# Scores of two blocks by row halves in turn, packed loads for short chunks, and two held conversions

## The chip, the cores and the metric

One core of one Trainium2 chip runs the whole program. The metric is the device time of one execution in microseconds (us); the median of several runs counts.

## The reference

Three steps, in this order, on a batch of 4 sequences of 576 tokens with 8 heads of 64:

```python
# 1. retention: attention with a decay in place of the softmax
scores = scale * (q @ k.T)
gamma = 1.0 - 2.0 ** (-5.0 - head)
ret = scores * where(i >= j, gamma ** (i - j), 0)
x = (ret @ v).reshape(2304, 512)
# 2. first feed-forward block, w_in 512x2048, w_out 2048x512
h = x @ w_in
y = (h * cos(h)) @ w_out
# 3. second feed-forward block, the same sizes
h = y @ w_in2
g = where(h >= 1, h, where(h <= -1, 0, (h + 1) ** 2 / 4))
out = g @ w_out2
```

The four weight matrices arrive with 64-bit elements; q, k and v are fp32.

## The kernel before, in words

**Precision.** The products of the feed-forward blocks are made of three matmuls each: every operand is split into a high and a low part (tiles with a leading index of 2, types fp32r), and high x high, high x low and low x high are added up. The weights are converted on the chip from the two 32-bit halves of each element. `begin` (L127) makes a scaled copy X of the upper half on ScalarE (L134); `convert` (L145) makes C from both halves on VectorE (L150 to L156), has `signed` (L139 to L143) work on X and W, copies the high part out on ScalarE (L158) and makes the low part on VectorE (L159). Raw weights come in by `load_raw` (L112) on the queue of SyncE (SP), into rotating buffers `raw` and `rsh` of two each; a later raw load waits until the conversion that reads the buffer is through.

**Chunks and blocks.** The 2304 tokens are cut into 5 blocks of 256, 512, 512, 512 and 512 tokens (L25) and, within sequences and blocks, into 20 chunks of 128 or 64 tokens (L49). Chunks 4, 6, 14 and 15 have 64 tokens: two in block 1, two in block 3. Blocks 0 and 1 together hold chunks 0 to 6, block 2 holds 7 to 10, block 3 holds 11 to 15 and block 4 holds 16 to 19.

**One chunk** (class `Chunk`, L251). `load` (L261) fetches q and k, transposed so that pairs of heads lie on 128 rows, then k and v by tokens, then a table of decays `pt`; for chunk 0 the last two go out on ScalarE's queue, otherwise all three on SP's. `prep` (L276) scales v by a table, on ScalarE in eight small copies for block 1 (L281), on VectorE for the others (L283). `scores` (L285) makes for each of four pairs of heads two matmuls over 64 rows each: the upper row half (j = 0) into PSUM bank S, the lower (j = 1) into bank O (in the start also y0 to y3; the profile names them bkS, bkO, bky). A fp32 matmul is two passes in the profile, so 16 per chunk. `masked` (L293) multiplies both banks with the mask on VectorE (R, L300). `full` (L305) then uses the two banks again for the carried state and for the state update, `inner` (L318) multiplies with v, `state` (L327) updates the state T, and `post` (L339) scales the result by `pt` into xs and splits it into the high and low part of x. So bank S comes free when the state is updated and bank O when xs is made.

**Order of the work.** The start (L640 to L680) loads chunks 0 to 6 and the first raw weights, then goes through the chunks; matmuls on zeros (`warm`, L633) fill TensorE early on. The conversion of the first W_in tile is called for after chunk 2 (L676), of the first W_out tile after chunk 4 (L678). From L740 on a loop over slots, each one column block of the hidden layer of one token block, runs the first product (`mm1`, L367), the activation, and two slots later the second product (`mm2`, L379). The chunks of blocks 2 to 4 are laid into the slots of the block before them by a plan (L586 to L621). The second feed-forward block follows at L774. The program's order sets priorities only: a scheduler of the framework walks each engine's instructions with its own estimate of their times and may put a ready one ahead of an earlier one that isn't. An order is forced with `behind(later, earlier)` (L94), which adds a dependency without a wait on the chip where both are on the same engine.

```python
for p in range(NP):
    for j in range(2):
        js = slice(j * D, (j + 1) * D)
        self.lastpe = PE.matmul(self.Z[j][:n, p * P:p * P + n], self.qk[js, 1, p, :n], self.qk[js, 0, p, :n], start=True, stop=True)
```

Of the kernel before, what the change touches and what calls it, by code (L numbers as in the profile page):

```python
# [13 lines left out]
AF = mybir.ActivationFunctionType  # L14
ALU = mybir.AluOpType
# [3 lines left out]
B, H, S, D = 4, 8, 576, 64  # L19
NT, DM, DFF = B * S, H * D, 2048  # L20
P = 128
KB = DM // P
NP = H // 2
# [25 lines left out]
def _chunks():  # L49
    out = []  # L50
    for b in range(B):
        t = 0
        while t < S:
            o, w = BLOCKS[_block_of(b * S + t)]
            n = min(P, S - t, o + w - (b * S + t))
            out.append((b, t, n))
            t += n
    return out


CHUNKS = _chunks()
NCH = len(CHUNKS)
# [3 lines left out]
def retention_moe_kernel(ctx: ExitStack, tc: tile.TileContext, qk, kv, win1, wout1, win2, wout2, mask, vtab, ptab, out):  # L66
    nc = tc.nc
    V, A, G, SY, PE = nc.vector, nc.scalar, nc.gpsimd, nc.sync, nc.tensor
# [14 lines left out]
    vtb = const.tile([P, NCH, H], F32, tag="vtb", name="vtb")  # L83
# [7 lines left out]
    def f(t):  # L91
        return t.bitcast(F32)

    def behind(later, earlier):  # L94
        tc.add_manual_dep(later.ins, earlier.ins.name, mybir.DependencyInfo(mybir.DependencyClass.NoSync, mybir.DependencyReason.SCHED_ONLY), reason="pace")

    def bank(tag):
        return psy.tile([P, 512], F32, tag=tag, name="bk" + tag)
# [28 lines left out]
    def begin(L, i, c, after=None, late=False):  # L127
        raw, raw2 = raws.pop((L, i, c))
        hi = raw[:, :, 1].bitcast(F32)
        if late:  # L130
            X, W = [wp.tile([P, DM], F32, tag=f"wo{k}", name="XW"[k - 1]) for k in (1, 2)]
        else:
            X, W = [cv.tile([P, DM], F32, tag=k, name=k) for k in "XW"]
        i0 = A.activation(X, hi, AF.Copy, scale=2.0 ** -112)  # L134
        if after is not None:
            behind(i0, after)
        return raw, raw2, X, W, late
# [7 lines left out]
    def convert(begun, o, after=None):  # L145
        raw, raw2, X, W, late = begun
        lo, hi = raw[:, :, 0], raw[:, :, 1]
        C = wp.tile([P, DM], I32, tag="wo3", name="C") if late else cv.tile([P, DM], I32, tag="C", name="C")
        if raw2 is not None:
            i0 = V.tensor_scalar(out=C, in0=raw2.bitcast(I32)[:, 1:1 + 2 * DM:2], scalar1=7, scalar2=None, op0=ALU.logical_shift_left)  # L150
        else:
            i0 = V.tensor_scalar(out=C, in0=hi, scalar1=23, scalar2=None, op0=ALU.logical_shift_left)
        if after is not None:
            behind(i0, after)
        if raw2 is None:
            V.scalar_tensor_tensor(out=C, in0=lo, scalar=9, in1=C, op0=ALU.logical_shift_right, op1=ALU.bitwise_or)  # L156
        signed(hi, X, W, 1)
        A.activation(o[:, 0, :], W, AF.Copy)  # L158
        return V.scalar_tensor_tensor(out=o[:, 1, :], in0=C, scalar=2.0 ** -43, in1=X, op0=ALU.mult, op1=ALU.mult)  # L159
# [3 lines left out]
    def make_wi1(c, begun, after=None):  # L163
        t = wr.tile([P, 2, DM], F32R, tag="wi", name="wi")
        convert(begun, t, after)
        SY.dma_start(out=wd[0, 0, c], in_=f(t))
        wi[0, c] = t

    def make_wo1(c, begun, after=None):
        t = wp.tile([P, 2, DM], F32R, tag=f"wo{c}", name=f"wo{c}")  # L170
        convert(begun, t, after)
        wo[0, c] = t
# [69 lines left out]
    CH = {}  # L242
# [8 lines left out]
    class Chunk:  # L251
# [9 lines left out]
        def load(self, other=None, homes=None):  # L261

            n = self.n
            if homes is None:
                both = ap.tile([P, 4, DM], F32, tag="qkv", name="qkv")
                self.qk, self.kv = both[:, 0:2], both[:, 2:4]
                self.pt = ap.tile([P, NP, P], F32, tag="pt", name="pt")
            else:
                self.qk, self.kv = [p_.tile([P, 2, DM], F32, tag=g_, name="qkv") for p_, g_ in homes[:2]]
                self.pt = homes[2][0].tile([P, NP, P], F32, tag=homes[2][1], name="pt")  # L270
            self.qk = self.qk.rearrange("p a (i m) -> p a i m", i=NP)
            SY.dma_start(out=self.qk, in_=qk[self.i])
            (other or SY).dma_start(out=self.kv[:n], in_=kv[self.i][:n])
            (other or SY).dma_start(out=self.pt[:, :, :n], in_=ptab[:, :, self.t:self.t + n])

        def prep(self):  # L276
            n = self.n
            v = self.kv[:n, 1, :].rearrange("p (h d) -> p h d", h=H)
            if self.blk == 1:
                for h in range(H):  # L280
                    A.activation(v[:, h, :], v[:, h, :], AF.Copy, scale=vtb[:n, self.i, h:h + 1])  # L281
                return
            V.tensor_tensor(out=v, in0=v, in1=vtb[:n, self.i, :].unsqueeze(2).to_broadcast([n, H, D]), op=ALU.mult)  # L283

        def scores(self):  # L285
            n = self.n
            self.Z = [bank(t) for t in self.banks]
            for p in range(NP):
                for j in range(2):
                    js = slice(j * D, (j + 1) * D)  # L290
                    self.lastpe = PE.matmul(self.Z[j][:n, p * P:p * P + n], self.qk[js, 1, p, :n], self.qk[js, 0, p, :n], start=True, stop=True)

        def masked(self, home=None):  # L293
            n = self.n
# [44 lines left out]
        def post(self):  # L339
            n = self.n  # L340
            xs = ap.tile([P, NP, P], F32, tag="xs", name="xs", bufs=1)
            V.tensor_tensor(
                out=xs[:, :, :n], in0=self.Z[1].rearrange("p (i m) -> p i m", i=NP)[:, :, :n],
                in1=self.pt[:, :, :n], op=ALU.mult)
            if self.off == 0:
                new_x(self.blk, BLOCKS[self.blk][1])
            xx = xhl[self.blk]
            os_ = slice(self.off, self.off + n)
            A.activation(xx[0][:, :, os_], xs[:, :, :n], AF.Copy)
            return V.tensor_tensor(out=xx[1][:, :, os_], in0=xs[:, :, :n], in1=f(xx[0][:, :, os_]), op=ALU.subtract)  # L350
# [272 lines left out]
    first = members[0] + members[1]  # L623
# [37 lines left out]
    for k, i in enumerate(first):  # L661
        c = CH[i]
        c.scores()
        c.masked((None, "wo2")[k % 2])
        if k < 2:
            warm(10, c.lastpe)
        if k + 1 < len(first):
            CH[first[k + 1]].prep()
        c.full()
        c.inner()  # L670
        c.state()
        if k < 2:
            warm(10, c.lastpe)
        lastpost = c.post()
        if k == 2:
            make_wi1(0, begin(0, 0, 0))  # L676
        if k == 4:
            make_wo1(0, begin(0, 1, 0))  # L678
            load_raw(0, 1, 1)
    make_wi1(1, begin(0, 0, 1))  # L680
    for p in range(-9, 0):
# [58 lines left out]
    for s in range(N1):  # L740
# [7 lines left out]
        after = lastpost if s <= pos_of[1, 0] else None  # L748
# [19 lines left out]
        q = 2 * (s - N1)  # L768
# [5 lines left out]
    for t, (sb, q, k) in enumerate(steps):  # L774
# [6 lines left out]
        n = 0  # L781
# [10 lines left out]
def _layout(q, k, v, moe_w_in, moe_w_out, moe2_w_in, moe2_w_out):  # L792
    import numpy as np

    qk = np.zeros((NCH, P, 2, NP, P), q.dtype)
    kv = np.zeros((NCH, P, 2, DM), q.dtype)
    for i, (b, t, n) in enumerate(CHUNKS):
        for j, a in enumerate((q, k)):
            qk[i, :, j, :, :n] = a[b, :, t:t + n, :].reshape(NP, 2, n, D).transpose(1, 3, 0, 2).reshape(P, NP, n)
        for j, a in enumerate((k, v)):  # L800
            kv[i, :n, j, :] = a[b, :, t:t + n, :].transpose(1, 0, 2).reshape(n, DM)

    def bits(w):
        w = np.ascontiguousarray(w)
        return w.view(np.int64)

    def wi(w):
        return bits(w.reshape(KB, P, NC, P).transpose(2, 1, 0, 3).reshape(NC, P, DM))

    def wo(w):  # L810
        return bits(w.reshape(NC, P, DM))

    g = np.array(GAMMA, np.float64)
    i = np.arange(S)
    start = np.array([t for b, t, n in CHUNKS])
    mask = np.triu(np.ones((P, P), np.float32))
    j = np.arange(P)[:, None, None] + start[None, :, None]
    vtab = (g[None, None, :] ** (-j)).astype(np.float32)
    pw = (g[:, None] ** i[None, :] / 8.0).astype(np.float32)
    ptab = np.repeat(pw.reshape(NP, 2, 1, S), D, axis=2).reshape(NP, P, S).transpose(1, 0, 2)  # L820
    return dict(qk=qk, kv=kv, win1=wi(moe_w_in), wout1=wo(moe_w_out), win2=wi(moe2_w_in), wout2=wo(moe2_w_out),
                mask=mask, vtab=vtab, ptab=ptab)

# [26 lines left out]
```

## Time and profile before

| | |
|---|---|
| median of 3 runs | 898.96 us (896.07 to 900.01) |
| the profiled execution | 897.41 us |
| its span, first to last instruction | 895.6 us |
| TensorE matmul busy (PE) | 869.6 us, 97% |
| TensorE weight load busy (PEld, beside PE) | 746.9 us, 83% |
| VectorE busy (DVE) | 632.2 us, 71% |
| ScalarE busy (ACT) | 481.8 us, 54% |
| mean granted TensorE clock | 0.991 of full |

The profile names an instruction by engine, line (L291 is line 291 of the kernel), operation and tiles, as out<-in. PE is TensorE's matmul, PEld its weight load, DVE VectorE, ACT ScalarE, POOL GpSimd; SPq and ACTq are the queues on which SyncE and ScalarE issue transfers. "idle before <-releaser" is how long an engine stood before an instruction and what released it. Matmuls are pipelined, so their durations overlap; the distance of their starts is what one costs.

### The profile page before, as it was taken

How to read it: one execution, taken by the hardware profiler on the slowest of the kernel's cores; microseconds unless marked ns; L12 is line 12 of the kernel's file. 1: busy time of each engine (PE TensorE's matmuls, PEld its weight loads, DVE VectorE, ACT ScalarE, POOL GpSimd, SP SyncE). 2: the span in 40 equal slices, each digit the busy share in tenths (PEclk: the TensorE clock that was granted, in tenths of full speed). 3: DMA queues.
4: the chain of work that ended last, by engine and by line, in shares of the span. 5: the costliest groups of instructions: out<-in, count | busy, mean ns of one | idle time of the engine just before them, and what ended most of it. 6: DMA issues, size and time to landing. Idle time of an engine off the chain costs nothing.

```text
span 895.6 us, 13569 instructions
## 1 busy us (share of the span) xinstructions
PE 869.6 (97%) x4876; PEld 746.9 (83%) x4876; DVE 632.2 (71%) x1152; ACT 481.8 (54%) x925; POOL 105.6 (12%) x82
## 2 busy tenths in 40 slices
PE   7888999999999999999999999999999999999997
PEld 6776888788888778788888899888888989898896
DVE  4797999765877785968889477685745667555554
ACT  3577988653566664666776644343433435423333
POOL 0022322200212221222232200000000000000000
PEclk9899999999999999999999999999999999999999
DMA  9968898855595968575986787676766765766431
GB/s 316 348 209 290 302 315 313 289 188 157 186 305 206 344 235 318 186 262 180 356 294 229 257 270 244 239 257 190 232 189 197 237 189 192 242 193 185 153 94 71
DMA packets 78114, 211.80 MB, mean 236 GB/s; under 512 B 9696, under 2 KB 21728, under 8 KB 78048
## 3 DMA queue, kind: packets, MB, share of 16 engines
q1 hardware_dynamic: 77088, 210.01, 69.8%
q10 hardware_dynamic: 960, 0.93, 0.3%
q8 instruction: 39, 0.64, 0.3%
q14 instruction: 27, 0.22, 0.1%
HBM read 170.02 MB, written 40.89 MB: 235 GB/s over the span
## 4 chain that ended last, share of the span: by engine, by line
PE 80%; DVE 7%; DMA 3%; ACT 3%; issue 2%; SPq 0%; DVEq 0%; ACTq 0%
PE hq L512 19%; PE h L376 14%; PE bky L391 6%; PE bky L392 6%; PE bky L393 6%; PE bky L565 5%; PE bky L564 5%; PE bky L566 5%; DVE W L142 1%; PE bkO L311 1%; PE bkO L376 1%; PE bkS L376 1%; PE bkS L565 1%; PE bkO L564 1%; PE bkO L324 1%
## 5 line engine op out<-in xcount | busy, mean ns | idle before, releaser
L512 PE MATMUL hq<-xc,wq 128*128 128x384 f32 x1008 | 198.4, 337 | 0.7 <-DVE sC L520 0.3
L376 PE MATMUL h<-xhl,wi 128*128 128x512 f32 (+1 forms) x864 | 194.2, 371 | 3.6 <-ACT wi L158 2.4
L512 PEld LDWEIGHTS hq<-xc,wq 128*128 128x128 f32 x1008 | 179.8, 188 | 12.8 <-DVE sC L520 0.6
L376 PEld LDWEIGHTS h<-xhl,wi 128*128 128x128 f32 x864 | 149.1, 189 | 33.2 <-ACT wi L158 3.5
L439 POOL TENSOR_TENSOR gl<-t,gh 128x512 fp32r<-128x512 f32 (+1 forms) x78 | 105.4, 1352 | 405.1 <-ACT gh L438 378.5
L438 ACT ACTIVATE gh<-t 128x384 fp32r<-128x384 f32 (+2 forms) x176 | 96.5, 549 | 56.0 <-DVE t L547 33.9
L546 ACT ACTIVATE t<-t,half 128x384 f32<-128x384 f32 x96 | 58.9, 615 | 107.2 <-DVE t L545 107.1
L391 PE MATMUL bky<-gh,wo 128*128 128x512 f32 x256 | 101.2, 395 | 2.4 <-ACT gh L438 2.4
L392 PE MATMUL bky<-gh,wo 128*128 128x512 f32 x256 | 100.1, 391 | 0.0
L393 PE MATMUL bky<-gl,wo 128*128 128x512 f32 x256 | 87.9, 390 | 0.0
L547 DVE TENSOR_TENSOR t<-t,sC 128x384 f32<-128x384 f32 x96 | 53.3, 556 | 33.3 <-ACT t L546 32.9
L564 PE MATMUL bky<-wo,gh 128*128 128x512 f32 x192 | 75.6, 394 | 0.2 <-ACT gh L438 0.2
L565 PE MATMUL bky<-wo,gh 128*128 128x512 f32 x192 | 75.6, 394 | 0.0
L431 ACT ACTIVATE t<-t 128x512 f32<-128x512 f32 (+1 forms) x80 | 46.9, 587 | 52.1 <-DVE t L426 51.9
L439 DVE TENSOR_TENSOR gl<-t,gh 128x384 fp32r<-128x384 f32 (+1 forms) x98 | 54.2, 556 | 18.0 <-ACT gh L438 17.8
L566 PE MATMUL bky<-wo,gl 128*128 128x512 f32 x192 | 61.0, 394 | 0.0
L545 DVE TENSOR_SCALAR t<-sC 128x384 f32<-128x384 f32 x96 | 34.4, 358 | 36.0 <-ACT sC L532 34.4
L391 PEld LDWEIGHTS bky<-gh,wo 128*128 128x128 f32 x256 | 48.0, 188 | 13.4 <-ACT gh L438 3.2
L392 PEld LDWEIGHTS bky<-gh,wo 128*128 128x128 f32 x256 | 48.1, 188 | 9.8 <-issue 0.3
L393 PEld LDWEIGHTS bky<-gl,wo 128*128 128x128 f32 x256 | 47.7, 188 | 9.7
L141 DVE TENSOR_SCALAR X<-X 128x512 int32<-128x512 int32 x64 | 30.7, 479 | 27.3 <-ACT X L134 27.1
L142 DVE SCALAR_TENSOR_TENSOR W<-raw,X 128x512 int32<-128x512 int32 x64 | 48.8, 762 | 1.1
(127 smaller groups left out, 1384.6 us busy)
## 6 DMA issues: line engine op xcount, KB each, us to landing
wq<-wq SPq DMA_DIRECT2D x72, 512.0 KB, 4.1
wi<-wd SPq DMA_DIRECT2D x48, 512.0 KB, 4.8
wo<-wd SPq DMA_DIRECT2D x48, 512.0 KB, 4.2
raw<-in_win_dram SPq DMA_DIRECT2D x32, 512.0 KB, 5.7
raw<-in_wout_dram SPq DMA_DIRECT2D x32, 512.0 KB, 5.6
qkv<-in_qk_dram SPq DMA_DIRECT2D x20, 512.0 KB, 6.3
wd<-wi SPq DMA_DIRECT2D x16, 512.0 KB, 4.4
wd<-cw SPq DMA_DIRECT2D x16, 512.0 KB, 5.5
```

Source lines behind the costliest of these rows:

```text
L142: V.scalar_tensor_tensor(out=Wi, in0=hi, scalar=-0x80000000, in1=Xi, op0=ALU.bitwise_and, op1=ALU.bitwise_or)
L376: PE.matmul(hp[s][:, :n], w[:, a, kb, :], x[b][:, kb, :], start=(i == 0), stop=(i == 3 * KB - 1))
L391: PE.matmul(o, w[:, 0, es], a, start=first and e % per == 0, stop=False, skip_group_check=True)
L392: PE.matmul(o, w[:, 1, es], a, start=False, stop=False, skip_group_check=True)
L393: PE.matmul(o, w[:, 0, es], b, start=False, stop=last, skip_group_check=True)
L438: A.activation(a, u, AF.Copy)
L439: eng.tensor_tensor(out=b, in0=u, in1=f(a), op=ALU.subtract)
L512: lastmm[0] = PE.matmul(o, w[:, a, kb, :], x[b][:, kb, :], start=first and i == 0, stop=i == 5, skip_group_check=True)
L546: A.activation(t, t, AF.Square, scale=0.5, bias=half)
L564: PE.matmul(y, a[:, js], w[:, 0, :], start=n == 0, stop=False)
L565: PE.matmul(y, a[:, js], w[:, 1, :], start=False, stop=False)
L566: PE.matmul(y, b[:, js], w[:, 0, :], start=False, stop=n == NC - 1)
```

## The change

- `load` takes q and k as one contiguous run of 2 x 4 x n elements per row, so a chunk of 64 tokens moves half of what it did; the decay table comes from an array with one packed copy per chunk, one run per row, where it was cut out of the whole table as four pieces of n elements.
- `prep` returns its last scaling for chunks of block 1.
- `scores` goes through the halves as (1, 0) instead of (0, 1), except in block 2, and puts each matmul behind the one before it, except in block 2.
- The first step (X) of the conversions called for after chunks 2 and 4 is put behind the last scaling of the next chunk, chunk 3 and chunk 5.
- The host's `_layout` lays out the arrays for it.

```diff
--- before.py
+++ after.py
@@ -268,27 +268,36 @@
             else:
                 self.qk, self.kv = [p_.tile([P, 2, DM], F32, tag=g_, name="qkv") for p_, g_ in homes[:2]]
                 self.pt = homes[2][0].tile([P, NP, P], F32, tag=homes[2][1], name="pt")
-            self.qk = self.qk.rearrange("p a (i m) -> p a i m", i=NP)
-            SY.dma_start(out=self.qk, in_=qk[self.i])
+
+            q = self.qk.rearrange("p a m -> p (a m)")[:, :2 * NP * n]
+            SY.dma_start(out=q, in_=qk[self.i][:, :2 * NP * n])
+            self.qk = q.rearrange("p (a i m) -> p a i m", a=2, i=NP)
             (other or SY).dma_start(out=self.kv[:n], in_=kv[self.i][:n])
-            (other or SY).dma_start(out=self.pt[:, :, :n], in_=ptab[:, :, self.t:self.t + n])
+            t = self.pt.rearrange("p i m -> p (i m)")[:, :NP * n]
+            (other or SY).dma_start(out=t, in_=ptab[self.i][:, :NP * n])
+            self.pt = t.rearrange("p (i m) -> p i m", i=NP)
 
         def prep(self):
             n = self.n
             v = self.kv[:n, 1, :].rearrange("p (h d) -> p h d", h=H)
             if self.blk == 1:
                 for h in range(H):
-                    A.activation(v[:, h, :], v[:, h, :], AF.Copy, scale=vtb[:n, self.i, h:h + 1])
-                return
+                    i0 = A.activation(v[:, h, :], v[:, h, :], AF.Copy, scale=vtb[:n, self.i, h:h + 1])
+                return i0
             V.tensor_tensor(out=v, in0=v, in1=vtb[:n, self.i, :].unsqueeze(2).to_broadcast([n, H, D]), op=ALU.mult)
 
         def scores(self):
             n = self.n
             self.Z = [bank(t) for t in self.banks]
+
+            self.lastpe = None
             for p in range(NP):
-                for j in range(2):
+                for j in (0, 1) if self.blk == 2 else (1, 0):
                     js = slice(j * D, (j + 1) * D)
+                    prev = self.lastpe
                     self.lastpe = PE.matmul(self.Z[j][:n, p * P:p * P + n], self.qk[js, 1, p, :n], self.qk[js, 0, p, :n], start=True, stop=True)
+                    if prev is not None and self.blk != 2:
+                        behind(self.lastpe, prev)
 
         def masked(self, home=None):
             n = self.n
@@ -341,7 +350,7 @@
             xs = ap.tile([P, NP, P], F32, tag="xs", name="xs", bufs=1)
             V.tensor_tensor(
                 out=xs[:, :, :n], in0=self.Z[1].rearrange("p (i m) -> p i m", i=NP)[:, :, :n],
-                in1=self.pt[:, :, :n], op=ALU.mult)
+                in1=self.pt, op=ALU.mult)
             if self.off == 0:
                 new_x(self.blk, BLOCKS[self.blk][1])
             xx = xhl[self.blk]
@@ -665,7 +674,7 @@
         if k < 2:
             warm(10, c.lastpe)
         if k + 1 < len(first):
-            CH[first[k + 1]].prep()
+            prepped = CH[first[k + 1]].prep()
         c.full()
         c.inner()
         c.state()
@@ -673,9 +682,9 @@
             warm(10, c.lastpe)
         lastpost = c.post()
         if k == 2:
-            make_wi1(0, begin(0, 0, 0))
+            make_wi1(0, begin(0, 0, 0, after=prepped))
         if k == 4:
-            make_wo1(0, begin(0, 1, 0))
+            make_wo1(0, begin(0, 1, 0, after=prepped))
             load_raw(0, 1, 1)
     make_wi1(1, begin(0, 0, 1))
     for p in range(-9, 0):
@@ -792,11 +801,11 @@
 def _layout(q, k, v, moe_w_in, moe_w_out, moe2_w_in, moe2_w_out):
     import numpy as np
 
-    qk = np.zeros((NCH, P, 2, NP, P), q.dtype)
+    qk = np.zeros((NCH, P, 2 * NP * P), q.dtype)
     kv = np.zeros((NCH, P, 2, DM), q.dtype)
     for i, (b, t, n) in enumerate(CHUNKS):
         for j, a in enumerate((q, k)):
-            qk[i, :, j, :, :n] = a[b, :, t:t + n, :].reshape(NP, 2, n, D).transpose(1, 3, 0, 2).reshape(P, NP, n)
+            qk[i, :, j * NP * n:(j + 1) * NP * n] = a[b, :, t:t + n, :].reshape(NP, 2, n, D).transpose(1, 3, 0, 2).reshape(P, NP * n)
         for j, a in enumerate((k, v)):
             kv[i, :n, j, :] = a[b, :, t:t + n, :].transpose(1, 0, 2).reshape(n, DM)
 
@@ -817,7 +826,10 @@
     j = np.arange(P)[:, None, None] + start[None, :, None]
     vtab = (g[None, None, :] ** (-j)).astype(np.float32)
     pw = (g[:, None] ** i[None, :] / 8.0).astype(np.float32)
-    ptab = np.repeat(pw.reshape(NP, 2, 1, S), D, axis=2).reshape(NP, P, S).transpose(1, 0, 2)
+    whole = np.repeat(pw.reshape(NP, 2, 1, S), D, axis=2).reshape(NP, P, S).transpose(1, 0, 2)
+    ptab = np.zeros((NCH, P, NP * P), np.float32)
+    for i, (b, t, n) in enumerate(CHUNKS):
+        ptab[i, :, :NP * n] = whole[:, :, t:t + n].reshape(P, NP * n)
     return dict(qk=qk, kv=kv, win1=wi(moe_w_in), wout1=wo(moe_w_out), win2=wi(moe2_w_in), wout2=wo(moe2_w_out),
                 mask=mask, vtab=vtab, ptab=ptab)
 
```

## Rows read from the trace of the kernel before

**Rows 1.** The page: the chain by engine, and one group of part 5.

```profile
PE 80%; DVE 7%; DMA 3%; ACT 3%; issue 2%; SPq 0%; DVEq 0%; ACTq 0%
...
L142 DVE SCALAR_TENSOR_TENSOR W<-raw,X 128x512 int32<-128x512 int32 x64 | 48.8, 762 | 1.1
```

**Rows 2.** Stretches: us, busy us of each engine (instructions), clock, DMA share, GB/s.

```profile
0.00:45.00 45.00, 35.82 (x436) 31.78 (x438) 28.67 (x58) 21.44 (x63) 1.22 (x5) 0.89 0.97 331
45.00:100.00 55.00, 47.49 (x269) 40.78 (x265) 48.86 (x95) 42.39 (x90) 14.12 (x9) 0.97 0.76 260
100.00:180.00 80.00, 76.71 (x436) 66.14 (x435) 71.46 (x122) 64.80 (x140) 22.46 (x19) 1.00 0.87 302
180.00:390.00 210.00, 209.62 (x1323) 168.86 (x1322) 157.52 (x275) 122.16 (x215) 36.85 (x27) 1.00 0.70 237
```

**Rows 3.** The same for the scores line L291 alone; last row sums 15 stretches.

```profile
211.10:213.05 1.95, 1.95 (x16) 1.83 (x16) 1.00 0.98 353
221.55:223.91 2.36, 2.21 (x16) 1.89 (x16) 1.00 0.60 153
243.56:243.97 0.41, 0.41 (x2) 0.29 (x2) 1.00 1.15 400
249.64:250.72 1.08, 1.08 (x14) 0.96 (x14) 1.00 0.91 322
267.60:268.21 0.61, 0.61 (x16) 0.54 (x16) 1.00 0.31 121
...
361.99:362.86 0.87, 0.87 (x12) 0.74 (x12) 1.00 0.00 0
...
383.04:383.69 0.65, 0.65 (x8) 0.52 (x8) 1.00 0.63 252
...
sum 12.81, PE 12.64 PEld 10.73; mean PE 0.84 PEld 0.72
```

**Rows 4.** Timeline of TensorE in two chunks of block 3: start, duration, instruction.

```profile
211.10 1.04 PE L291 MATMUL bkS<-qkv 64*128 64x128 f32 x7
...
212.18 0.94 PE L291 MATMUL bkO<-qkv 64*128 64x128 f32 x7
...
249.64 0.37 PE L291 MATMUL bkO<-qkv 64*128 64x128 f32 x1
249.64 0.37 PE L291 MATMUL bkS<-qkv 64*128 64x128 f32 x1
```

**Rows 5.** DMA queues from 0 to 45 us: packets, MB, share of 16 engines.

```profile
q1 hardware_dynamic: 6634, 13.88, 90.1%
q10 hardware_dynamic: 960, 0.93, 6.2%
```

**Rows 6.** Timeline of ScalarE from 0 to 50 us.

```profile
12.11 0.71 ACT L134 ACTIVATE X<-raw 128x512 f32<-128x512 f32 x1 [9.43 <-DMA raw<-in_win_dram]
...
19.83 2.02 ACT L281 ACTIVATE qkv<-qkv,vtb 128x64 f32<-128x64 f32 x8 [1.68 <-DMA qkv<-in_kv_dram]
...
26.88 0.65 ACT L134 ACTIVATE X<-raw 128x512 f32<-128x512 f32 x1
29.70 2.02 ACT L281 ACTIVATE qkv<-qkv,vtb 128x64 f32<-128x64 f32 x8 [2.17 <-DMA qkv<-in_kv_dram]
```

**Rows 7.** Two stretches, then rows of VectorE's, SP's and TensorE's timelines.

```profile
20.00:26.00 6.00, 2.57 (x48) 2.20 (x46) 1.11 (x3) 3.41 (x15) 0.00 (x0) 1.00 1.06 319
26.00:33.00 7.00, 5.97 (x52) 5.21 (x52) 6.89 (x15) 4.51 (x15) 0.00 (x0) 0.54 1.03 322
...
25.94 0.43 DVE L152 TENSOR_SCALAR C<-raw 128x512 int32<-128x512 int32 x1 [4.57 <-DMA raw<-in_wout_dram]
...
24.89 0.34 SPq L118 DMA_DIRECT2D raw<-in_win_dram  x1
...
29.74 0.56 SPq L274 DMA_DIRECT2D pt<-in_ptab_dram  x1
...
33.02 0.51 PE L376 MATMUL h<-xhl,wi 128*128 128x256 f32 x1
```

## The prediction

> **What bounds the kernel now.** I read the chain that ended last first [rows 1]: 80% of it is TensorE. That share is an average over two regimes, so next come the stretches [rows 2]. From 180 to 390 us, where the chunks of the last two blocks are scored, TensorE is busy 209.62 of 210 us at full clock: whatever leaves TensorE's queue there leaves the time. From 0 to 45 us it is busy 35.82 of 45 at a granted clock of 0.89, while the DMA engines are at 0.97 and 331 GB/s: the start is paced by transfers. Between 45 and 180 us VectorE (48.86 of 55, then 71.46 of 80) and TensorE share the load. Behind 390 us nothing is edited.
>
> Then the scores line alone, in 15 stretches that hold every score matmul of blocks 3 and 4 [rows 3]: each runs from its first score to the next other matmul, and together they last 12.81 us. The timeline of two chunks [rows 4] shows why some are cheap. At 211.10 seven passes go to bank S and then, from 212.18, seven to bank O, one behind the other (one pair meets in between); at 249.64 an O pass and an S pass start together, each on its own row half, and two cost what one costs.
>
> For the start I read the DMA queues [rows 5], ScalarE's order [rows 6] and six rows on what is due when [rows 7].
>
> **Part 1, scores by halves, O first, chained.** Removed: no instruction. Moved: in blocks 0, 1, 3 and 4 each chunk's eight matmuls (16 passes) keep the order O, S, O, S, and none may go before O is free. A long chunk (128 tokens) in one piece: four pairs take 0.65, six 0.87 [rows 3], so a pair adds 0.11, and eight take 0.87 + 2 x 0.11 = 1.09. A short chunk (64) is 0.61 and is already paired. Blocks 3 and 4 hold seven long and two short: 7 x 1.09 + 2 x 0.61 = 8.85 us against 12.81 now, 4.0 less. Of that, 0.86 come from the chunk at 211.10 (1.95) and 1.27 from the one at 221.55 (2.36). Three chunks put one S matmul alone ahead of the rest (0.41 at 243.56; two more like it), some 0.4 each. Two are cut in two though both banks are free (0.65 at 383.04 and as much again 3 us later; 0.87 at 361.99 and a rest of two pairs). I see nothing in the edit that forbids these last cuts, some 0.2 each, so I leave them in: **3.6 us**, all on the path by [rows 2]; the ends are 4.0 and rival C. Blocks 0 and 1 wait for transfers: nothing, covered by the DMA engines at 0.97; if that cover is gone, 0.2 per cut. The wait that the chain adds, S behind O's release, holds back S matmuls alone; behind them on TensorE stands the next hidden-layer group, which needs neither bank, and the masks, which VectorE forms of both banks, aren't complete before O's scores now either.
>
> **Part 2, packing.** Two short chunks lie in the start and move 256 KB less of q and k each. The SP queue moved 13.88 MB in 90.1% of 45 us [rows 5], 342 GB/s, so 0.76 us each, 1.5 together. Tables: the same bytes in a quarter of the pieces. ScalarE's queue, a mix with many table pieces, moved 0.93 MB in 6.2% of 45 us, 333 GB/s, so the gain on a 256-KB table may be as little as 0.02 us; from above, a table's issue holds SP 0.56 us where a load in whole rows holds it 0.34 [rows 7], 0.22 less. Seven tables lie in the start: 0.1 to 1.5 us. I take 0.1 each, 0.7, near the lower end, since that one is a price of the transfer itself. Sum 2.2, bounds 1.6 to 3.0. The two short chunks of block 3 load beside TensorE's 209.62 of 210: nothing; TensorE would have to wait for them first, which it doesn't.
>
> On the tables the Trainium skill speaks against the change: "DMA: Bandwidth & Descriptors", section Specifications, lets 512 bytes be enough for line rate. By it the five long tables, cut into 512-byte pieces, would give nothing, and part 2 would be, an estimate, some 1.7 us. The nearness of 333 to 342 GB/s agrees with it, though no row has a table by itself.
>
> **Part 3, the two first conversions held.** Only the first step of each, ScalarE's scaled copy X, gets the new order; VectorE's steps on C don't. For the first W_in tile X runs at 12.11 now, ahead of two scalings; it moves behind chunk 3's scaling, which ends at 19.83 + 2.02 = 21.85 [rows 6]. Its four VectorE steps (at most 4 x 0.76 = 3.0 us by [rows 1]) fall into 20 to 26 us, where VectorE is busy 1.11 of 6 [rows 7]; the tile is due at 33.02, at the first hidden-layer matmul. Nothing. For the first W_out tile X moves from 26.88 behind chunk 5's scaling, 29.70 + 2.02 = 31.72, or 29.7 if the transfers come 2 us earlier. Here the cover is thin: VectorE is busy 6.89 of 7 from 26 to 33. Bounds 0 and +3.0 us; I take 0, the lower, since the tile's first use is the second product, which no chunk before 33.02 can reach, and the steps that leave 26 to 33 let masks go that wait there. On SP's queue the fifth raw load, at 24.89 [rows 7], reuses the first tile's buffer and holds block 2's loads behind it: the buffer now comes free some 2 us after 21.85, so nothing, at worst 1 us. What isn't cured: a VectorE step on C stood until 25.94, 4.57 us, for a raw transfer, with masks behind it [rows 7]; it comes perhaps 1.5 us earlier by part 2.
>
> **Sum.** The profiled execution took 897.41 us (895.6 of it the span), 1.55 under the median of 898.96 (runs from 896.07 to 900.01). Part 1 -3.6; part 2 -2.2, of which 2.0 reach 45 us and so the end, because the stretch behind is a chain of conversions whose work isn't changed; part 3 nothing. That is 897.41 - 5.6 = 891.8, or **893.4** against the median.
>
> **Rivals.**
> B, *the start gives nothing back, or costs.* Part 3 lays up to 3.0 us of VectorE work behind a stretch that is full, and what the transfers gain is spent waiting for conversions. For it: VectorE's 71.46 of 80 later on. Against: chunk 5's scaling comes earlier too. 893.4 + 2.0 without part 2, + 5.0 with all of part 3: 895.4 to 898.4.
> C, *the chain is scattered*, the slower side. The new order is only a rank on TensorE's queue; other groups may come between the links, as one came between 243.56 and 249.64. A matmul alone costs 0.41, eight alone 3.3. All seven long chunks scattered, the two short ones between 0.61 and 3.3 each: 24.3 to 29.7 instead of 12.81, so +11.5 to +16.9, less 2.0: 908 to 914. It is slower than the bound once the nine chunks together pass 12.81 + 2.0 + 4.5 = 19.3 us. Against it: dependent matmuls that accumulate, twelve in a row, mostly stay together in the trace.
> D, *the change doesn't do what it says*: long chunks still go in two pieces, as at 361.99, some 1.3 each: 7 x 1.3 + 1.22 = 10.3, only 2.5 gained; with part 2, 894.5, and 897.0 if no chunk gains.
>
> **How the numbers follow.** Half a per cent, 4.5 us, is what a measurement of this kernel can tell from no change. My forecast 0.50, its own span 890 to 895 (4.0 and 3.0 at the one end, 3.0 and 1.0 at the other); B 0.22; D 0.18; C 0.10. Faster by over 4.5 us means under 894.5: nearly all of the forecast and a little of D, 0.51. Slower is most of C, 0.09. The rest, 0.40, is the same. The range leaves out C, reaches over B and D, and takes in the spread of the runs, about 2 us to either side: 888 to 900.
>
> **What would show it.** Right: in the changed profile the O and S passes of every chunk of blocks 3 and 4 start in pairs, O first, and their stretches sum to 8.9 to 9.3 us; the first hidden-layer matmul stands some 2 us before 33.02; the first X follows a scaling that ends near 21. Wrong: stretches that still sum to over 12, scores that lie one by one between other matmuls, or a stretch from 45 to 180 us that takes longer than now, by which the start's gain would be lost.

## The result, and the profile after

| | before | after |
|---|---|---|
| median | 898.96 us (896.07 to 900.01) | 892.18 us (889.65 to 892.85) |
| profiled execution | 897.41 us | 892.85 us |
| its span | 895.6 us | 891.1 us |

The medians stand 6.8 us apart; the ratio is 0.9916, 95% interval 0.9893 to 0.9940. The two profiled executions are only 4.6 us apart: the changed kernel's is the slowest of its five runs. The forecast was 893.4. The sum was close, but three of its terms were not, and they cancelled by luck; the experiments below show which.

The page of the changed kernel, the chain by engine; it answers to [rows 1] and still names TensorE first:

```profile
PE 80%; DVE 6%; DMA 4%; ACT 3%; issue 1%; SPq 0%; DVEq 0%; ACTq 0%
```

The four stretches of the changed kernel, columns as in [rows 2]:

```profile
0.00:45.00 45.00, 33.97 (x422) 30.23 (x424) 28.66 (x58) 22.15 (x66) 1.13 (x5) 1.00 0.92 329
45.00:100.00 55.00, 49.76 (x297) 42.48 (x293) 51.98 (x98) 43.85 (x92) 15.15 (x10) 0.97 0.76 266
100.00:180.00 80.00, 77.03 (x429) 65.69 (x428) 68.30 (x119) 62.91 (x136) 21.84 (x19) 1.00 0.88 302
180.00:390.00 210.00, 207.58 (x1348) 168.95 (x1348) 162.47 (x279) 125.07 (x220) 36.34 (x28) 1.00 0.70 240
```

In the first stretch the DMA engines fell from 0.97 to 0.92, so the transfers no longer fill it. TensorE's 33.97 us for 35.82 come at a mean granted clock of 1.00 for 0.89 and are no measure of work saved. In the last stretch TensorE still bounds the time, but it now stands still for 2.4 us, 0.2 before. Its waits from 176 to 382 us in the changed kernel (line, releaser: us in total, times, longest), all but the last new:

```profile
PE h L385 <- DVE t L455: 1.4, 1, 1.4
PE bkO L298 <- DVE xs L351: 0.8, 1, 0.8
PE bkS L325 <- DVE R L309: 0.2, 1, 0.2
```

The scores line of the changed kernel (L298, which was L291), the stretches that answer to [rows 3]:

```profile
209.98:211.07 1.09, 1.09 (x16) 0.97 (x16) 1.00 0.96 380
223.56:224.42 0.86, 0.86 (x10) 0.73 (x10) 1.00 0.56 195
230.08:230.72 0.64, 0.64 (x6) 0.52 (x6) 1.00 0.38 147
247.16:248.25 1.09, 1.09 (x16) 0.97 (x16) 1.00 1.01 385
264.69:265.31 0.62, 0.61 (x16) 0.55 (x16) 1.00 0.00 0
280.81:281.42 0.61, 0.61 (x16) 0.54 (x16) 1.00 1.05 423
293.83:294.25 0.42, 0.41 (x2) 0.29 (x2) 1.00 1.04 400
299.91:300.78 0.87, 0.86 (x10) 0.74 (x10) 1.00 0.92 311
306.44:306.86 0.42, 0.42 (x4) 0.30 (x4) 1.00 0.61 166
329.16:329.58 0.42, 0.42 (x2) 0.29 (x2) 1.00 0.96 361
337.96:339.05 1.09, 1.09 (x14) 0.96 (x14) 1.00 1.03 421
358.21:358.85 0.64, 0.64 (x8) 0.52 (x8) 1.00 0.00 0
361.80:362.45 0.65, 0.65 (x8) 0.52 (x8) 1.00 0.01 3
381.61:382.70 1.09, 1.09 (x16) 0.97 (x16) 1.00 0.84 319
```

They sum to 10.51 us against 12.81. An uncut long chunk costs 1.09, as worked out; but only three of the seven are uncut (209.98, 247.16, 381.61). The four others come in two or three pieces, 3.6 to 8.8 us apart: feed-forward matmuls that the program calls earlier become ready in between and go first. At 293.83 and 329.16 one O matmul now stands alone ahead of the rest, where it was one S matmul before. Because of these cuts the stretches gained 2.3, not 3.6 or 4.0. From block 2's first score (at 182.30 us before, 180.32 now) to the end of block 4's last the two profiled executions took 204.98 and 202.38 us: 2.6 less. That is 2.3 from the stretches, less 2.2 for the two new waits, and 2.5 by which other matmuls between these scores became cheaper by the distance of their starts; why they did was not looked into. Behind block 4's last score both took 508.4 us.

ScalarE in the start of the changed kernel, for [rows 6]:

```profile
19.36 2.02 ACT L285 ACTIVATE qkv<-qkv,vtb 128x64 f32<-128x64 f32 x8 [2.33 <-DMA qkv<-in_kv_dram]
21.28 0.66 ACT L134 ACTIVATE X<-raw 128x512 f32<-128x512 f32 x1
...
27.46 2.02 ACT L285 ACTIVATE qkv<-qkv,vtb 128x64 f32<-128x64 f32 x8 [1.90 <-DMA qkv<-in_kv_dram]
29.39 0.67 ACT L134 ACTIVATE X<-raw 128x512 f32<-128x512 f32 x1
```

Both X stand right behind their scalings, at 21.28 and 29.39, where the forecast put them (near 21; 29.7). TensorE's first hidden-layer matmul and the fifth raw load, for [rows 7]:

```profile
25.61 0.38 PE L385 MATMUL h<-xhl,wi 128*128 128x256 f32 x1 [1.75 <-ACT wi L158]
...
30.50 0.53 SPq L118 DMA_DIRECT2D raw<-in_win_dram  x1
```

The matmul came 7.4 us earlier than at 33.02, not 2, and had to wait for the held tile; the next ones stood at 38.50 instead of 40.63, the first of 512 columns at 49.55 instead of 49.81, so the head start was gone by 50 us. The raw load went out 5.6 us later than at 24.89. Of the prediction's signs of being right, the first X came where it said; the stretches (8.9 to 9.3 us) and the first matmul did not.

### The profile page after: what moved, and what is told of

It is laid out like the page before. It is cut to its first block, busy times and chain, and to the rows that moved or that the text cites. A ratio compares the mean times of both kernels' runs of the same rounds, so it can differ in the third digit from the quotient of the medians.

```text
span 891.1 us, 13579 instructions
## 1 busy us (share of the span) xinstructions
PE 863.8 (97%) x4876; PEld 742.7 (83%) x4876; DVE 633.9 (71%) x1152; ACT 482.2 (54%) x925; POOL 105.5 (12%) x82
## 4 chain that ended last, share of the span: by engine, by line
PE 80%; DVE 6%; DMA 4%; ACT 3%; issue 1%; SPq 0%; DVEq 0%; ACTq 0%
PE hq L521 19%; PE h L385 15%; PE bky L400 6%; PE bky L402 5%; PE bky L401 5%; PE bky L573 5%; PE bky L574 5%; PE bky L575 5%; DMA raw<-in_wout_dram 2%; PE bkO L298 1%; PE bkS L574 1%; PE bkO L573 1%; PE bkO L575 1%; PE bkO L385 1%; PE bkS L385 1%
## 5 line engine op out<-in xcount | busy, mean ns | idle before, releaser
L142 DVE SCALAR_TENSOR_TENSOR W<-raw,X 128x512 int32<-128x512 int32 x64 | 52.3, 818 | 1.2
L141 DVE TENSOR_SCALAR X<-X 128x512 int32<-128x512 int32 x64 | 28.9, 451 | 26.8 <-ACT X L134 26.8
```

## The experiments

The three parts were taken one by one, then in pairs, then split further. Ratios are to the kernel before on the same chip, with 95% intervals; each time given is the kernel's median, and each difference in us is its ratio on 898.5. The expectations also name the moment of block 2's first score, 182.30 us in the kernel before; it is given from the profiled execution, a single one, and so is a hint only.

**Scores edit alone.** The kernel before with the new order in blocks 0, 1, 3 and 4:

```diff
-                for j in range(2):
+                for j in (0, 1) if self.blk == 2 else (1, 0):
...
+                    if prev is not None and self.blk != 2:
+                        behind(self.lastpe, prev)
```

> The kernel before with the edit of the scores alone. Theory 1 (the parts add up, and scores are worth what their stretches lose on TensorE's queue behind 182 us): the stretches of blocks 3 and 4 sum to about 10.5 us instead of 12.81, the time falls by 2.3 to 2.6 us, ratio 0.997, and block 2's first score stays at 182.3. Theory 2 (any moved instruction reorders the start, and that decides): block 2's first score moves by 1 us or more in either direction.

Measured: 892.00 us, 0.9937 (0.9921 to 0.9952): -5.7 us, more than theory 1's 2.3 to 2.6 and the prediction's 3.6. Its stretches in blocks 3 and 4 sum to 10.47, so that place gives 2.3 here as well. Block 2's first score stood at 180.51, 1.8 us earlier, which is theory 2's sign. The rest has to come from blocks 0 and 1.

**Scores edit in blocks 3 and 4 only:**

```diff
-                for j in range(2):
+                for j in (0, 1) if self.blk <= 2 else (1, 0):
...
+                    if prev is not None and self.blk > 2:
+                        behind(self.lastpe, prev)
```

> The kernel before with the scores edit in blocks 3 and 4 alone. Theory: the 2.3 us behind 182 stay, and the 1.8 us that the whole scores edit won ahead of 182 are gone: block 2's first score at 182.3, time 2.3 to 2.6 us below before, ratio 0.997. Rival: block 2's first score near 180.5 all the same.

Measured: 895.65 us, 0.9969 (0.9952 to 0.9985): -2.8 us, stretches 10.47. So blocks 3 and 4 give about what their stretches lose, and about 2.9 us of the edit come from blocks 0 and 1, by the difference of two intervals that just touch. Block 2's first score stood at 185.82 in the profiled execution, not at 182.3; the last section comes back to this.

**Packing alone** (long, so its core: q, k and the table are read as the first columns of rows made ready per chunk):

```diff
-            SY.dma_start(out=self.qk, in_=qk[self.i])
+            SY.dma_start(out=q, in_=qk[self.i][:, :2 * NP * n])
...
-            (other or SY).dma_start(out=self.pt[:, :, :n], in_=ptab[:, :, self.t:self.t + n])
+            (other or SY).dma_start(out=t, in_=ptab[self.i][:, :NP * n])
```

> The kernel before with packed loads and tables alone. Theory 1: transfers of the start land earlier, block 2's first score comes 2.0 us before 182.3 and the time falls by 2.0, ratio 0.998. Theory 2 (what the transfers gain is spent waiting for conversions by 50 us): block 2's first score within 0.5 us of 182.3, ratio 1.000.

Measured: 893.46 us, 0.9958 (0.9939 to 0.9976): -3.8 us, against 2.0 in the forecast; block 2's first score stood at 176.86. The next two kernels take one half of it each: the first pair of lines above, or the second.

> The kernel before with q and k of short chunks packed, the tables as before. If bytes count: 2 x 0.76 us less to move in the start, 1.5 us at block 2's first score and in the time, ratio 0.998. If packing works by moving the third conversion out of a full stretch of VectorE: that conversion's low part ends 2 us or more before 44.5, and block 2's first score comes as much or more before 182.3.

> The kernel before with the tables packed, q and k as before. By the page's rule that 512 bytes are enough for line rate: only two short tables gain, under 0.5 us, ratio 0.9995 or above. If small pieces cost more than the rule says: seven tables at 0.1 to 0.3 us, the loads behind them go out 1 to 2 us earlier, block 2's first score 1 us or more before 182.3, ratio 0.998 or less.

Measured: q and k alone 894.59 us, 0.9959 (0.9941 to 0.9977), -3.7 us; the tables alone 892.69 us, 0.9938 (0.9916 to 0.9959), -5.6 us. The two do not add up: 9.3 us as a sum, 3.8 together, and within the intervals both together give no more than either. Block 2's first score stood at 182.41 with q and k alone, no earlier than before, and at 177.50 with the tables alone. The tables' gain is real and contradicts "nothing". The DMA queues from 0 to 45 us in the kernel with packed tables alone, columns as in [rows 5]:

```profile
q1 hardware_dynamic: 4468, 14.39, 90.2%
q10 hardware_dynamic: 576, 0.93, 5.6%
```

ScalarE's queue carries one 256-KB table, and its bytes are the same: 6.2% became 5.6% of 45 us, 0.27 us for that table (0.18 in the kernel after, at 5.8%). SP's queue rose from 342 to 14.39 MB / (0.902 x 45 us) = 354 GB/s. It is so in every kernel: with the tables in pieces (five kernels) ScalarE's queue shows 6.1 to 6.3% and SP's 339 to 345 GB/s, with packed ones (nine) 5.6 to 5.9% and 352 to 369. I had put 0.1 us on a table.

**The two holds alone, and with packing.** The kernel before, then the kernel before with packing, each with

```diff
-            make_wi1(0, begin(0, 0, 0))
+            make_wi1(0, begin(0, 0, 0, after=prepped))
...
-            make_wo1(0, begin(0, 1, 0))
+            make_wo1(0, begin(0, 1, 0, after=prepped))
```

> The kernel before with the two held conversions alone. Theory 1: nothing, ratio 0.9995 to 1.001, though the first hidden-layer matmul may move. Theory 2: the hold is what let the first hidden-layer matmul go at 25.6 instead of 33.0, and the 2 us at 182 are its own: 2 us less, ratio 0.998.

> The changed kernel with the scores as before. Theory 1: 2.0 us less than before, all of it at block 2's first score (180.3), and 2.5 more than the changed kernel: ratio 0.998. Theory 2: not the sum of the packing alone and the hold alone, by over 1 us.

Measured: holds alone 898.82 us, 1.0011 (0.9997 to 1.0025), no change within the interval, which allows a cost of up to 2.2 us. The first hidden-layer matmul stood at 31.48, so theory 2 fell. Packing with holds 896.56 us, 0.9985 (0.9970 to 1.0000), against 0.9958 without: +2.4 us, by two intervals that overlap a little. Block 2's first score stood at 182.29, not at 180.3. Beside packing the holds cost most of what it gave; that they cost less without it is likely, but the intervals leave it open.

**The change without the holds, and with one of them.** The kernel after, with both of the lines above undone, then with the W_out line alone undone, then with the W_in line alone undone:

> The changed kernel without the two held conversions. Theory 3 (the hold moves two conversions' VectorE work behind 20 us, where that engine is full, and the third conversion, which is not held, ends 3 to 5 us later; the packing by itself is worth some 5 us at block 2's first score): the third conversion's low part ends near 40 us instead of 43.1, block 2's first score stands near 177 instead of 180.3, and the time is 3 us below the changed kernel: ratio to before 0.989. Rival (the order of the start is a matter of chance, and each kernel draws its own): block 2's first score anywhere from 177 to 183, ratio 0.990 to 0.996, without a tie to the third conversion.

> The changed kernel with the hold on the first W_in tile alone. Theory 3: its four VectorE steps fit into 20 to 26 us, where the engine is nearly idle, so it costs little: block 2's first score within 1 us of the kernel without any hold. Rival: as bad as both holds together, since the later W step holds back the fifth raw load on SP's queue.

> The changed kernel with the hold on the first W_out tile alone. Theory 3: this one pushes the third conversion, and costs the 3 us: block 2's first score near 180. Rival: nothing, 177.

Measured: without holds 888.93 us (888.01 to 889.37), 0.9892 (0.9875 to 0.9909), the fastest kernel here, 2.2 us under the change by the ratios; with the hold on W_in 891.34, 0.9921 (0.9903 to 0.9939); on W_out 892.01, 0.9934 (0.9909 to 0.9958). Either hold alone costs 2.6 or 3.8 us, both together 2.2: within the intervals the same. The intervals of no hold and both holds overlap. The kernels with no hold and with one ran on the same chip, and there each of the 12 runs with one hold was slower than the slowest of the 5 without (889.44 against 889.37 us at the closest). Block 2's first score stood at 174.41 without holds, at 177.44 with W_in's and at 179.87 with W_out's. So theory 3 was right on the time without holds and on W_out, and wrong on W_in, whose hold it said would cost little. VectorE's last step (L159) of the first W_in tile, the first W_out tile and the second W_in tile in the kernel without holds:

```profile
15.64 0.69 DVE L159 SCALAR_TENSOR_TENSOR wi<-C,X 128x512 fp32r<-128x512 int32 x1
...
30.18 0.69 DVE L159 SCALAR_TENSOR_TENSOR wo<-C,X 128x512 fp32r<-128x512 int32 x1
...
38.39 0.68 DVE L159 SCALAR_TENSOR_TENSOR wi<-C,X 128x512 fp32r<-128x512 int32 x1
```

The same three steps in the kernel after:

```profile
25.16 0.68 DVE L159 SCALAR_TENSOR_TENSOR wi<-C,X 128x512 fp32r<-128x512 int32 x1
...
35.01 0.68 DVE L159 SCALAR_TENSOR_TENSOR wo<-C,X 128x512 fp32r<-128x512 int32 x1
...
42.43 0.68 DVE L159 SCALAR_TENSOR_TENSOR wi<-C,X 128x512 fp32r<-128x512 int32 x1
```

Held, the first tile ends 9.5 us later, W_out's 4.8 and the second W_in tile 4.0. With W_in's hold alone the last two end at 33.18 and 40.80, with W_out's alone at 37.66 and 41.40. Stretches of the start show where VectorE lost the time, columns as in [rows 2] (VectorE is the third engine). The kernel without holds:

```profile
10.00:20.00 10.00, 8.12 (x136) 7.19 (x134) 8.31 (x15) 5.59 (x18) 0.00 (x0) 1.00 1.04 369
20.00:26.00 6.00, 0.68 (x16) 0.57 (x16) 2.38 (x5) 4.03 (x14) 0.00 (x0) 0.81 1.03 353
26.00:33.00 7.00, 6.91 (x71) 6.59 (x71) 6.82 (x15) 5.61 (x19) 0.00 (x0) 0.68 1.02 383
33.00:45.00 12.00, 11.49 (x169) 10.08 (x167) 11.75 (x25) 6.78 (x17) 0.73 (x1) 1.00 0.77 303
```

The kernel after:

```profile
10.00:20.00 10.00, 8.69 (x102) 7.77 (x101) 5.95 (x11) 3.93 (x14) 0.00 (x0) 1.00 1.04 367
20.00:26.00 6.00, 3.47 (x59) 3.04 (x57) 3.84 (x8) 5.00 (x17) 0.00 (x0) 1.00 1.04 349
26.00:33.00 7.00, 4.44 (x68) 3.97 (x67) 5.70 (x12) 5.54 (x19) 0.00 (x0) 1.00 1.02 371
33.00:45.00 12.00, 10.18 (x142) 8.94 (x144) 11.33 (x24) 6.18 (x16) 0.93 (x1) 1.00 0.75 289
```

By 45 us VectorE has done 8.31 + 2.38 + 6.82 + 11.75 = 29.26 us of work without holds and 26.82 with them: 2.4 us less. The hold empties 10 to 20 us, the gap at 20 to 26 takes up only 1.5 of it, and from 26 to 33 VectorE stands again, in the kernel after for the second X, which now comes at 29.39 instead of 24.62:

```profile
30.09 0.43 DVE L141 TENSOR_SCALAR X<-X 128x512 int32<-128x512 int32 x1 [1.25 <-ACT X L134]
```

With W_in's hold alone that X comes at 25.03, and VectorE stands there all the same, for a raw transfer:

```profile
31.02 0.43 DVE L152 TENSOR_SCALAR C<-raw 128x512 int32<-128x512 int32 x1 [1.16 <-DMA raw<-in_win_dram]
```

The missing 2.4 us are owed behind 45 us, where VectorE is busy 51.98 of 55. The pair with packing shows the same, 28.42 and with holds 26.62, and so does W_in's hold alone, 26.80; the pair without packing, where no cost was clear of the noise, shows no loss, 26.61 and 26.70. So the loss goes with the cost in four pairs of kernels; with W_out's hold alone it is 1.4 (27.88), less than that kernel's cost. It is not enough as an account: the kernel with only q and k packed has done hardly more by 45 us (26.75) than the kernel before (26.61) and is still 3.7 us faster. That the lost work is what the holds cost is my reading, and no run shows it by itself. The granted clock is no explanation: from 26 to 33 us its mean was 0.68 in the faster of the two and 1.00 in the slower.

**Block 2 in the new order too**, on the kernel without holds:

```diff
-                for j in (0, 1) if self.blk == 2 else (1, 0):
+                for j in (1, 0):
...
-                    if prev is not None and self.blk != 2:
+                    if prev is not None:
```

> The changed kernel without the holds and with block 2's scores also O first and chained. Its four long chunks take 4 x 1.09 = 4.4 us instead of 7.94. If TensorE's own time is the limit there: 3.5 us less than without it, ratio 0.985. If the chunks of block 2 follow each other by masks and states and not by TensorE: the stretch from block 2's first score to block 3's keeps its 28.8 us, and the time stays.

Measured: 889.87 us, 0.9901 (0.9884 to 0.9919), no gain on 0.9892. Block 2's score stretches fall from 7.94 to 7.17 only, not to 4.4, so the first theory was hardly put to the test. TensorE's waits from 176 to 206 us, where block 2 is scored (line, releaser: us in total, times, longest):

```profile
PE bkS L325 <- DVE R L309: 1.8, 1, 1.8
PE bky L400 <- ACT gh L447: 1.7, 1, 1.7
PE bkO L298 <- DVE xs L351: 0.8, 1, 0.8
PE bkO L320 <- DVE R L309: 0.8, 1, 0.8
```

These are 5.1 us. Without this edit block 2 shows 0.2. From its first score to block 3's first it now takes 30.8 us instead of 29.7: there VectorE and ScalarE, with masks, xs and activations, end last, not TensorE.

**No cuts at all.** On the kernel without holds, each chunk's first score in blocks 3 and 4 also goes behind the last feed-forward matmul that was called before it:

```diff
+                    if prev is None and self.blk > 2:
+                        behind(self.lastpe, lastff[0])
...
-                PE.matmul(hp[s][:, :n], w[:, a, kb, :], x[b][:, kb, :], start=(i == 0), stop=(i == 3 * KB - 1))
+                lastff[0] = PE.matmul(hp[s][:, :n], w[:, a, kb, :], x[b][:, kb, :], start=(i == 0), stop=(i == 3 * KB - 1))
...
-            PE.matmul(o, w[:, 0, es], b, start=False, stop=last, skip_group_check=True)
+            lastff[0] = PE.matmul(o, w[:, 0, es], b, start=False, stop=last, skip_group_check=True)
```

> The changed kernel without the holds, and with each chunk's first score in blocks 3 and 4 put behind the last feed-forward matmul called for before it, so that no such matmul can come between. Its score stretches sum to 7 x 1.09 + 2 x 0.61 = 8.85 us instead of 10.48. If TensorE is the limit there: 1.6 us less than without this edit, ratio to before 0.987. Rival: the chunks then start later and their masks make TensorE wait, and nothing or less is gained.

Measured: 890.67 us, 0.9918 (0.9897 to 0.9940), not faster than 0.9892. The stretches sum to 8.85, exactly the forecast for uncut chunks, 1.6 less than with cuts; but from block 2's first score to block 4's last it took 201.97 us instead of 202.41, 0.4 less. The wait that costs TensorE most in these 202 us here:

```profile
PE h L388 <- DVE t L458: 3.6, 3, 1.6
```

The same wait in the kernel without this edit:

```profile
PE h L385 <- DVE t L455: 1.4, 1, 1.4
```

The cuts were not mere losses: with the scores last, hidden-layer groups wait 2.2 us more for an activation in this trace. The 4.0 us at the far end of part 1 could not be had this way.

## Why the prediction was right in the sum and wrong in its terms

| term | forecast | measured |
|---|---|---|
| scores, blocks 3 and 4 | -3.6 | -2.8 (stretches -2.3) |
| scores, blocks 0 and 1 | 0 | about -2.9 |
| packing | -2.0 | -3.8 (-5.5 to -2.2) |
| holds, beside packing | 0 | +2.2 to +2.4 (alone +1.0, -0.3 to +2.2) |
| sum | -5.6 | -7.3; the change itself -7.5 by its ratio, -6.8 by medians |

The +2.2 is read from the change itself, so the sum checks nothing by it; with the +2.4 of the pair without the scores edit the sum is -7.1.

**Scores, blocks 3 and 4: the mechanism right in the main, the size off.** 1.09 and 0.61 per uncut chunk stood. Device time less the moment of block 2's first score is 715.0 to 717.1 us in the profiled executions of the six kernels with the old order in blocks 3 and 4, and 712.3 to 714.0 in the eight with the new one: this gain lies where the prediction put it. The term that was mis-sized is "some 0.2 each" for two cuts: there were four cut chunks, and they took 1.50, 1.71, 1.51 and 1.29, so 0.2 to 0.6 over 1.09 each. "I see nothing in the edit that forbids these last cuts" was true of all seven chunks and was applied to two; before, a third chunk was already cut that way (its six passes at 302.82 and eight at 309.13), which I counted only as one with a matmul ahead. Rival D's price of 10.3 was the better one.

"Holds back S matmuls alone" failed as well. Block 3's first scores, where S went ahead of O at 211.10, now wait for O with TensorE standing still, 0.8 us. So of the 0.86 us that I took from this chunk nearly nothing is left. That the time still fell by more than the stretches is owed to the other matmuls, which I had not priced.

**Scores, blocks 0 and 1: "nothing, covered by the DMA engines at 0.97" failed.** A share of DMA time over 45 us can hide moments in which a chunk's scores are late for something else, VectorE's masks perhaps; no run isolates it. In the kernel with the scores edit alone the second W_in tile's last step ends at 41.7 us, in the kernel before at 44.5 and with the edit in blocks 3 and 4 only at 44.1. What within the start passes that on to the end was not settled.

**Packing: "0.1 each, near the lower end" failed.** The one long table that can be read by itself gave 0.2 to 0.27 us of its queue; an estimate for seven like it is 1.3 to 1.9. The Trainium skill, "DMA: Bandwidth & Descriptors", section Specifications, takes pieces of 512 bytes as enough for line rate; these runs speak against it: that table in rows of 2 KB instead of 512 bytes, the same bytes, went faster by 0.2 us, SP's queue went faster in every kernel with packed tables, and the kernel with these alone was faster by 5.6 us (3.7 to 7.5). That the end gains more than the transfers lose is open; so is why q and k on top of the tables add nothing.

**Holds: "Nothing" and "I take 0, the lower" failed, as rival B said.** Its mechanism, VectorE's work laid behind a full stretch, fits the stretches of the start; its bound of +3.0 was nearly met. I had checked the first X against the due time of its tile (33.02) and against room at 20 to 26. But, if the reading above is right, room was needed for work that had to be done by 45, not for one tile. For the first tile the step that failed is "due at 33.02": the scheduler moved that use to 25.61, and TensorE then waited 1.75 us for the tile. The cover I named "thin" for W_out did not hold. "At worst 1 us" for the fifth raw load failed as well: with both holds it went out at 30.50, behind two chunks' loads that the scheduler had put ahead of it, and with W_out's alone at 22.8. So this delay is not what W_out's hold costs; for W_in's hold (31.07) it is not ruled out.

**The rivals.** C did not come: no chunk went one by one. D was half right (cuts), B right on the holds, with a mechanism that fits. The sum stood by luck: 0.8 us too much in blocks 3 and 4 and 2.2 to 2.4 missed for the holds met 2.9 and 1.8 missed elsewhere.

The end of the second W_in tile's last step sorts the kernels: 44 us or later, ratios from 0.9969 to 1.0011; 41 to 43.1, from 0.9916 to 0.9959; under 40, from 0.9892 to 0.9958. Eight of the kernels also have the new order in blocks 3 and 4. Less its gain (0.0031), the groups are 0.9985 to 1.0011, 0.9947 to 0.9968 and 0.9923 to 0.9958: the first stands apart, the other two still overlap. In each pair where holds cost over 2 us this step ended 2.4 to 5.0 us later, and the holds alone left it where it was (44.3 for 44.5). That suits this tile as the start's bound better than the sums of VectorE's work do, but moving that one step alone was not tried.

## What to carry to other kernels

Before an operation is delayed "into a gap", add up the work of the engine that follows it up to the next full stretch: what the gap cannot start, because its input is held too or not there yet, is owed later, and a quicker neighbour (here the transfers) may bring the price out. Measure such a delay by itself, beside the other parts of the change and without them. A share of 0.97 of one resource does not make every other engine's time there free. And where a scheduler fills TensorE by readiness, cuts in a burst cost some tenths each, yet forbidding them buys a wait elsewhere: price both.

## What the runs showed that I had not expected

Two profiled executions of the same order can part by several microseconds in the start. The kernel with the scores edit in blocks 3 and 4 only has every engine's order as in the kernel before until block 3 is scored, yet block 2's first score stood at 185.82 instead of 182.30 us. One GpSimd subtraction, the matmul behind it, and VectorE's first idle time after 53.69 in that kernel:

```profile
53.69 9.45 POOL L444 TENSOR_TENSOR gl<-t,gh 128x256 fp32r<-128x256 f32 x1 [10.10 <-ACT gh L443]
...
63.19 0.58 PE L398 MATMUL bkS<-gl,wo 128*128 128x256 f32 x1 [5.56 <-POOL gl L444]
...
64.14 0.52 DVE L451 SCALAR_TENSOR_TENSOR t<-t,hs 128x256 f32<-128x256 f32 x1 [1.58 <-ACT t L437]
```

The same subtraction in the kernel before, and VectorE's first idle time after it began:

```profile
55.05 0.96 POOL L439 TENSOR_TENSOR gl<-t,gh 128x256 fp32r<-128x256 f32 x1 [11.12 <-ACT gh L438]
...
56.05 0.69 DVE L426 SCALAR_TENSOR_TENSOR t<-t,hs 128x512 f32<-128x512 f32 x1 [0.64 <-ACT t L425]
```

And the stretch around it in the first of the two, columns as in [rows 2]:

```profile
53.00:63.00 10.00, 4.64 (x27) 3.94 (x27) 9.56 (x21) 7.53 (x16) 9.31 (x1) 0.95 0.73 251
```

Ten times as long, 9.45 us for 0.96, while VectorE was busy 9.56 of 10 us with 21 instructions, and TensorE waited 5.56 us. VectorE's share alone does not tell the two apart (9.36 of these 10 us before); its first gap does. In the kernel before VectorE fell idle at 55.41 and the subtraction ended at 56.01; here VectorE fell idle at 62.56 and it ended at 63.14, both 0.6 us later. The kernel with the holds alone shows it too: 10.49 us, ended 0.6 us after VectorE fell idle at 63.17, and TensorE waited 4.8 us for it. So this subtraction seems to have waited for a gap of VectorE's. It is no rule (the first kernel's subtraction at 66.23 took 0.73 us with VectorE busy throughout), and no run moves that gap by itself. The Trainium skill, "SBUF — State Buffer", section Who interferes with whom, says that GpSimd and VectorE share a port pair under an exclusive lock, which in VectorE's two-port modes the first to issue holds for its whole instruction; that GpSimd waits for VectorE agrees with these rows, but here it seems to have waited through many instructions in a row. It is not all of the 3.5 us at block 2's first score: TensorE lagged the kernel before by 5.9 us at 63 to 69 us, by 1.3 at 84, and by 2.2 again at 170. As the same order met this wait in one execution and not in the other, single traces of these kernels can't price the start: the prices above go by medians of several runs, and moments of the start are hints only. Whether the subtraction on VectorE would take this out was not tried.
